# Transposes of k ahead of both of their copies, and the last turned tokens two channel products later

## The chip, the cores and the metric

One core of a Trainium2 chip runs the whole program. The metric is device time in microseconds (us), median of the timed runs. Every run of this study was in the fast state. "The profile" is one execution recorded by the hardware profiler; its engines are PE (TensorE), PEld (TensorE's weight loads), DVE (VectorE), ACT (ScalarE), POOL (GpSimd) and SP. L514 is line 514 of the kernel's source.

## The reference

An RWKV-6 recurrence over 4 batches, 8 heads, 768 steps and head size 48, then an MLP mixer on its result.

```python
for t in range(S):                       # state: (B, H, D, D)
    cur = einsum('bhd,bhe->bhde', u * k[t], v[t])
    y[t] = einsum('bhd,bhde->bhe', r[t], state + cur)
    state = w[t] * state + einsum('bhd,bhe->bhde', k[t], v[t])
x = y as (B, S, H*D)                     # (4, 768, 384)
h = relu(x^T @ w_tok1) @ w_tok2          # tokens, 768 -> 256 -> 768
u = x + h^T
out = u + relu(u @ w_ch1) @ w_ch2        # channels, 384 -> 1536 -> 384
```

## The kernel before

The recurrence is done in 12 units of 256 tokens (two chunks of 128), three units to a batch. A unit's `tokens` transposes k for both chunks (8 transposes, 2 copies); `carry` makes from it the products `kv_ps`, which VectorE adds to the state.

```python
def tokens():                                     # one of the pieces of a unit
    ...
    L["kT"] = apool.tile([128, UC, A, 128], f32, name="kT", bufs=1)
    both = ps_g.tile([128, 2, 512], f32, name="gram").rearrange("p c (a t) -> p c a t", a=A)
    for c in range(UC):                           # UC = 2 chunks, A = 4 pairs of heads
        ps = both[:, c]                           # one PSUM bank for each chunk
        for a in range(A):
            pe.transpose(ps[:, a, :], k_[:, ts(c * A + a, 128)], ident)
        act.copy(L["kT"][:, c], ps)

def carry():
    L, vt = live[i], vs[i]
    kv = L["kv"] = ps_a.tile([128, 2, 512], f32, name="kv_ps", tag="a")
    ...         # pe.matmul(kv[...], L["kT"][...], vt[...])
```

Tiles carry their dependences: whoever reads a tile waits for what was written into it, and a later write waits for an earlier read. `gram` is one tile, with both banks in it.

The mixer of a batch adds the token product to x (`back`), turns 128 tokens of x (`turn`), and multiplies with the channel weights (`up`, 256 tokens at a time, the segment `s`):

```python
def back(c):
    ...         # h_ps = wtok2 x h1
    dve.tensor_add(x[:, c, :], x[:, c, :], ps)                 # L624

def turn(c):
    ...         # ps = xT_ps, in pool "a" in the first and last batch, else a gram tile
    for m in range(DM // 128):
        pe.transpose(ps[:, m, :], xs[bt][:, c, ts(m, 128)], ident)
    act.copy(xT[:, :, ts(c, 128)], ps)

turned = [(1.3, lambda: back(0))]
for c in range(1, C):                             # C = 6
    turned += [(1.3, lambda c=c: back(c)), (0.6, lambda c=c: turn(c - 1))]
turned.append((0.6, lambda: turn(C - 1)))
```

The opening also converts the weights, which come as 64-bit floats, in VectorE steps:

```python
def load():     # sp.dma_start(d64[...], src)     into the tile scratch, L207
def take():
    dve.tensor_scalar(e, top, 0x7FF0, None, op0=ALU.bitwise_and)      # L210, first to read the load
    ...         # L211, L212
def add(): ...                                    # L215
def scale(): ...                                  # L218
def put(): ...                                    # L223
```

And this is how the order on the engines comes about:

```python
for bt in range(B):
    if bt == 0:                                   # units 3 to 5 beside it; a scheduler decides
        to_ch = [whole(e[n < 2:]) for n, e in enumerate(to_ch)]
        late(in_turn[dve.engine], dve, lambda: emit(woven(turned, to_ch[:2])))
        ...
    else:
        hiddens, pieces, ups, downs = mixing(bt)
        pieces = [(c * 0.5, f) for h in hiddens for c, f in h] + [(c * 0.3, f) for c, f in pieces]
        for s in range(S // SEG):
            pieces += ups[s] + downs[s]
    ...
        strict(*(f for _, f in woven(att, pieces)))   # bt 1 and 2: fixed order on PE, DVE and ACT
```

Units 0 to 2 (the opening) and 3 to 5 (beside the first batch's mixer) are ordered in good part by the scheduler, units 6 to 11 (the **woven batches**) by the program. `late(mark, engine, f)` makes an engine's instructions of `f` stand behind `mark` in its queue.

## Time and profile before

| | before |
|---|---|
| device time, median | 601.02 us (600.21 to 602.07, 3 runs) |
| span of the profiled run, its mean granted clock | 603.1 us, 0.977 (this run took 605.13 us, 4.1 above the median) |
| TensorE busy | 565.3 us, 94% |
| VectorE busy | 391.8 us, 65% |
| waits of TensorE's matmuls, 240 to 480 us | 4.9 us, in 8 gaps |

TensorE is the bound, and its gaps are what can be won. The prediction below shows the views that carry this. Two stretches that it doesn't show are needed later. First, TensorE's timeline at the unit with the least to do between the transposes and their reader, `kv_ps`. The columns are start, duration (us), engine, line, operation, out<-in, shape, records in the row, and in brackets the idle time before with what ended it.

```profile
473.58 0.60 PE L514 MATMUL gram<-ident,rk 128*128 128x128 f32 x4
474.86 0.66 PE L514 MATMUL gram<-ident,rk 128*128 128x128 f32 x4 [0.68 <-ACT kT L515]
475.35 1.46 PE L642 MATMUL z_ps<-xT,wch 128*128 128x256 f32 x6
476.74 1.14 PE L524 MATMUL kv_ps<-vt,kT 64*64 64x48 f32 x48
```

Between the first transpose and `kv_ps` lie 3.16 us, 1.28 of them to the second four. Second, VectorE's timeline in the opening, where the mixer of the first batch begins (the same columns):

```profile
86.97 1.22 DVE L218 SCALAR_TENSOR_TENSOR scratch<-scratch 128x1024 f32<-128x1024 f32 x1
88.11 0.68 DVE L343 TENSOR_TENSOR decay<-w 112x512 f32<-112x512 f32 x1
88.71 0.55 DVE L624 TENSOR_TENSOR x<-x,h_ps 128x384 f32<-128x384 f32 x1
89.17 1.28 DVE L223 SCALAR_TENSOR_TENSOR wch<-x,scratch 128x512 uint32<-128x512 uint32 x2
90.38 0.55 DVE L624 TENSOR_TENSOR x<-x,h_ps 128x384 f32<-128x384 f32 x1
90.84 0.69 DVE L210 TENSOR_SCALAR scratch<-scratch 128x1024 uint16<-128x1024 uint16 x1
```

The first two sums into x (L624) come ahead of the first step (L210) of the next conversion, and nothing waits. TensorE's first transposes of x follow the first sum at 89.31 us.

### The profile page before, as it was taken

The numbers are of one execution on the slowest core, as the hardware profiler recorded it, in microseconds if no ns is written. First come the engines' busy times: TensorE is split into PE (matmuls) and PEld (weight loads), VectorE is DVE, ScalarE is ACT, GpSimd is POOL, SyncE is SP. The second block draws the span as 40 slices with busy tenths as digits, with TensorE's granted clock in tenths as the row PEclk, the third lists the DMA queues.
The fourth block names the chain that finished last, engine by engine and source line by source line (L and its number), as shares of the span: only waits on it lengthen the run. The fifth ranks groups of instructions, "written<-read, shape, count | busy, mean of one in ns | idle before, by whom it ended". The sixth has DMA issues, their size and how long they took to land.

```text
span 603.1 us, 17493 instructions
## 1 busy us (share of the span) xinstructions
PE 565.3 (94%) x7828; PEld 483.0 (80%) x7828; DVE 391.8 (65%) x729; ACT 180.1 (30%) x452; POOL 9.3 (2%) x46
## 2 busy tenths in 40 slices
PE   3767899999999999999999999999999999999997
PEld 2757657776897886689898896789899886898987
DVE  5779599998785696577778865677867142040403
ACT  6154435432224422322223302322313212303020
POOL 4000000000010000000000000000000000000000
PEclk9997599989999999999999999999999999999999
DMA  8525555630223315113232122010110000000000
GB/s 340 194 69 158 158 150 190 192 107 2 80 82 86 90 42 171 27 32 104 79 107 80 28 82 79 1 54 16 41 54 28 1 27 0 1 18 10 26 1 26
DMA packets 22969, 45.74 MB, mean 76 GB/s; under 512 B 2512, under 2 KB 14928, under 8 KB 22896
## 3 DMA queue, kind: packets, MB, share of 16 engines
q1 hardware_dynamic: 22752, 44.64, 23.6%
q8 instruction: 61, 1.00, 0.7%
q14 instruction: 12, 0.10, 0.1%
q10 hardware_dynamic: 144, 0.00, 0.0%
HBM read 39.91 MB, written 4.72 MB: 74 GB/s over the span
## 4 chain that ended last, share of the span: by engine, by line
PE 81%; DVE 11%; issue 3%; ACT 3%; DMA 2%; SPq 0%; DVEq 0%; ACTq 0%
PE z_ps L642 29%; PE q_ps L676 23%; PE h_ps L622 5%; PE h_ps L615 4%; PE gram L308 4%; PE gram L386 3%; PE kv_ps L524 2%; PE y_ps L576 2%; PE h_ps L652 2%; DVE rk L342 2%; PE gram L514 2%; PE y_ps L563 2%; PE xT_ps L634 1%; PE gram L302 1%; DMA x<-in_w_ch_dram 1%
## 5 line engine op out<-in xcount | busy, mean ns | idle before, releaser
L642 PE MATMUL z_ps<-xT,wch 128*128 128x256 f32 x864 | 196.3, 384 | 2.0 <-ACT z L644 2.0
L642 PEld LDWEIGHTS z_ps<-xT,wch 128*128 128x128 f32 x864 | 162.6, 191 | 25.3 <-ACT z L644 3.0
L644 ACT ACTIVATE z<-z_ps 128x256 f32<-128x256 f32 x144 | 55.0, 383 | 181.6 <-PE z_ps L642 181.4
L676 PE MATMUL q_ps<-wch,z 128*128 128x192 f32 x528 | 93.4, 328 | 0.0
L676 PEld LDWEIGHTS q_ps<-wch,z 128*128 128x128 f32 x528 | 86.5, 190 | 1.3
L676 PE MATMUL q_ps<-scratch,z 128*128 128x192 f32 x396 | 69.3, 328 | 0.0
L676 PEld LDWEIGHTS q_ps<-scratch,z 128*128 128x128 f32 x396 | 64.6, 190 | 0.4
L308 PEld LDWEIGHTS gram<-rk 48*64 48x64 f32 x1536 | 33.4, 171 | 9.3 <-issue 4.3
L308 PE MATMUL gram<-rk 48*64 48x32 f32 x1536 | 35.7, 250 | 5.4 <-issue 2.6
L342 DVE TENSOR_TENSOR rk<-rk,decay 112x1024 f32<-112x1024 f32 x24 | 29.4, 1223 | 16.1 <-PE gram L302 9.9
L720 DVE TENSOR_TENSOR z<-z 128x768 f32<-128x768 f32 x9 | 8.6, 953 | 47.4 <-ACT z L644 47.4
L412 DVE COPY_PREDICATED at<-mask,gram 128x384 f32<-128x384 uint8 (+2 forms) x72 | 34.5, 481 | 1.4
L622 PE MATMUL h_ps<-h,wtok 128*128 128x384 f32 x96 | 35.0, 491 | 0.0
L615 PE MATMUL h_ps<-x,wtok 128*128 128x384 f32 x96 | 35.0, 518 | 0.0
L624 DVE TENSOR_TENSOR x<-x,h_ps 128x384 f32<-128x384 f32 x24 | 13.2, 551 | 31.4 <-PE h_ps L622 31.4
L342 DVE TENSOR_TENSOR rk<-rk,w 112x1024 f32<-112x1024 f32 x24 | 29.3, 1223 | 6.3 <-PE gram L308 6.1
L615 PEld LDWEIGHTS h_ps<-x,wtok 128*128 128x128 f32 x96 | 18.7, 201 | 11.5 <-issue 0.6
L622 PEld LDWEIGHTS h_ps<-h,wtok 128*128 128x128 f32 x96 | 16.5, 190 | 9.8 <-ACT h L617 2.6
L514 PE MATMUL gram<-ident,rk 128*128 128x128 f32 x96 | 17.0, 305 | 7.6 <-ACT kT L515 7.1
L580 ACT COPY x<-y_ps 128x384 f32<-128x384 f32 x12 | 5.7, 479 | 59.2 <-PE y_ps L576 59.2
L544 DVE TENSOR_TENSOR state<-state,kv_ps 128x192 f32<-128x192 f32 x40 | 14.1, 353 | 11.7 <-PE kv_ps L524 10.5
L686 DVE TENSOR_TENSOR o<-x,z 128x192 f32<-128x192 f32 x11 | 3.9, 355 | 27.2 <-ACT z L685 27.2
(110 smaller groups left out, 650.5 us busy)
## 6 DMA issues: line engine op xcount, KB each, us to landing
rk<-in_rkw_dram SPq DMA_DIRECT2D x36, 192.0 KB, 3.4
x<-in_w_ch_dram SPq DMA_DIRECT2D x10, 512.0 KB, 4.5
vt<-in_v_dram SPq DMA_DIRECT2D x12, 384.0 KB, 4.3
out_dram<-o SPq DMA_DIRECT2D x24, 192.0 KB, 1.9
rp<-in_near_dram SPq DMA_DIRECT2D x12, 384.0 KB, 3.6
scratch<-in_w_ch_dram SPq DMA_DIRECT2D x8, 512.0 KB, 4.7
w<-in_rkw_dram SPq DMA_DIRECT2D x18, 192.0 KB, 3.6
rk<-in_rkw_dram SPq DMA_DIRECT2D x6, 512.0 KB, 6.5
```

The costliest lines, as they stand in the source:

```text
L308: fours(lambda q, j, rows, cols: pe.matmul(g[cols, q, ts(ca, 32)], k_[rows, ds(ca * 128 + j * T, T)], right[rows, ts(2 * ca + j, 32 // b), ...
L342: dve.tensor_mul(halves, halves, by)
L386: fours(lambda q, j, rows, cols: pe.matmul(g[cols, q, ts(a, 96)], k_[rows, ds((c * A + a) * 128 + j * T, T)], L["far", c][rows, ts(2 * a + ...
L412: dve.copy_predicated(out=to[:, :, :, (q + 1) * b:], data=got[:, :, :, first * b:first * b + n], mask=masks4[l][:, q].unsqueeze(1).unsquee ...
L514: pe.transpose(ps[:, a, :], k_[:, ts(c * A + a, 128)], ident)
L544: dve.tensor_add(new, new, got)
L615: pe.matmul(sums[i], wtok1[:, c, ts(i, 128)], xs[bt][:, c, :], start=(c == 0), stop=(c == C - 1))
L622: pe.matmul(ps, wtok2[:, i, ts(c, 128)], h1[:, i, :], start=(i == 0), stop=(i == DTOK // 128 - 1))
L624: dve.tensor_add(x[:, c, :], x[:, c, :], ps)
L642: pe.matmul(ps, wch1[:, m, ts(jt, 128)], xT[:, m, ts(s, SEG)], start=(m == 0), stop=(m == DM // 128 - 1))
L644: act.activation(zs[s][:, jt, :], ps, AF.Relu)
L676: pe.matmul(ps, a[:, j, :], b[:, j, :], start=(j == 0), stop=(j == HJ - 1))
```

## The change

Part one: all eight transposes of a unit are issued, then both copies, so that TensorE doesn't stand between the two fours. Part two: in the woven batches, the last turned tokens of a batch come after two channel products that don't need them, so that VectorE has time to finish the last sum into x.

```diff
             for c in range(UC):
-                ps = both[:, c]
                 for a in range(A):
-                    pe.transpose(ps[:, a, :], k_[:, ts(c * A + a, 128)], ident)
-                act.copy(L["kT"][:, c], ps)
+                    pe.transpose(both[:, c, a, :], k_[:, ts(c * A + a, 128)], ident)
+            for c in range(UC):
+                act.copy(L["kT"][:, c], both[:, c])
@@
             pieces = [(c * 0.5, f) for h in hiddens for c, f in h] + [(c * 0.3, f) for c, f in pieces]
+
+            *pieces, last = pieces
+            ups[0].insert(2, last)
             for s in range(S // SEG):
```

## The prediction

> **What bounds the kernel now.** I began with the busy shares on the page of the kernel before, then read its chain of work that ended last, then its groups.
>
> ```profile
> PE 565.3 (94%) x7828; PEld 483.0 (80%) x7828; DVE 391.8 (65%) x729; ACT 180.1 (30%) x452; POOL 9.3 (2%) x46
> ...
> PEclk9997599989999999999999999999999999999999
> ...
> PE 81%; DVE 11%; issue 3%; ACT 3%; DMA 2%; SPq 0%; DVEq 0%; ACTq 0%
> ...
> L514 PE MATMUL gram<-ident,rk 128*128 128x128 f32 x96 | 17.0, 305 | 7.6 <-ACT kT L515 7.1
> ```
>
> TensorE (PE) is busy 94% of the span and holds 81% of the chain that ended last. From about 150 us on its granted clock is full. So an idle TensorE gap removed after that point should shorten the run one for one, unless the gap comes back elsewhere. The last line is the group the change is about: 96 transposes of k (12 units of 8), before which TensorE sat idle 7.6 us, 7.1 of it for the ScalarE copy kT.
>
> Next I asked for TensorE's waits between 240 and 480 us alone, the two batches in which attention and mixer are woven in a fixed order. The columns are total us, times, longest.
>
> ```profile
> PE gram L514 <- ACT kT L515: 4.1, 6, 0.7
> PE xT_ps L634 <- DVE x L624: 0.8, 2, 0.4
> ```
>
> These are the only two waits that the answer names for the matmul row, and the change aims at exactly these two. Now the timeline of TensorE around one of them (start, duration, what, idle before):
>
> ```profile
> 378.19 0.49 PE L634 MATMUL xT_ps<-ident,x 128*128 128x128 f32 x3
> 378.52 0.60 PE L514 MATMUL gram<-ident,rk 128*128 128x128 f32 x4
> 379.80 0.66 PE L514 MATMUL gram<-ident,rk 128*128 128x128 f32 x4 [0.68 <-ACT kT L515]
> 380.29 1.46 PE L622 MATMUL h_ps<-h,wtok 128*128 128x384 f32 x4
> ...
> 383.20 0.49 PE L634 MATMUL xT_ps<-ident,x 128*128 128x128 f32 x3
> 384.10 0.52 PE L634 MATMUL xT_ps<-ident,x 128*128 128x128 f32 x3 [0.41 <-DVE x L624]
> 384.46 2.76 PE L642 MATMUL z_ps<-xT,wch 128*128 128x256 f32 x12
> ```
>
> Four transposes are issued, then TensorE stands until the first copy has ended, then the other four follow. Five microseconds later the last three token transposes of the batch stand until VectorE has added the last product to x.
>
> **What the Trainium skill says.** (1) "PSUM — Partial Sum Buffer", section "PSUM bank collisions raise a hardware error", has as its rule: "Semaphore-guard PSUM by bank × quadrant (by bank is the simple version), not by address." The tile of the transposes is two banks, one per chunk, so the second four write a bank that the first copy doesn't read. The chip does not ask for this wait; it comes from the dependences being taken for the tile as a whole. The order listing of the changed program agrees: the second four lose their wait on ScalarE, and the first copy now waits for all eight. (2) "TensorE: Matmul & The Clock Gate", section "Part 4: PE-mode transpose", gives about 275 ns for one transpose in a kernel. The trace has 272 to 273 ns as the median of L514, so it agrees; but in a row they start 0.11 us apart (three from 378.19 to 378.52), and this spacing is what counts here. (3) "Perfetto Trace Analysis", section "Identifying Performance Opportunities" (its Optimization Strategy): consistent bubbles, the same gap repeating on the engine that should be saturated, are to be looked for. The 0.68 us above repeats in five of the six units and is 0.73 in the sixth.
>
> **Part one, transposes ahead of both copies.** It adds and removes no instruction. Start to start, the second four follow the first four by 1.33 us once and by 1.28 us five times in the woven batches, 7.73 us in all. Four transposes at 0.11 need 0.44, 2.6 us for six units. So 7.73 - 2.6 gives **5.1 us** of gap. All of it is on TensorE at full clock.
>
> Does it come back at kv_ps (L524), which reads both copies? A copy takes 0.58 us and starts 0.07 us after the last transpose ends, so both are done about 1.2 us later, some 2.3 us after the first transpose starts. Eight transposes take 0.9 us, and the order listing puts between them and kv_ps at least one z_ps group: six records at 0.216 us, 1.3 us, and 0.33 us of issue that kv_ps shows anyway. That is 2.5 us, so no wait in the woven batches, narrowly in the unit at 473 us and widely in the others.
>
> In the first batch's second half (units at 160, 185 and 213 us) other products already lay between the two fours, so there was nearly no wait to lose. There the listing leaves only four q_ps matmuls (two records each, 0.16 us a record, 1.3 us) after the eight. At 160 us I expect about nothing. At 213 us the copies now stand behind two rp copies that wait for VectorE until about 214.6 us, so kv_ps comes with fewer products done: a loss of **0.5 us**.
>
> The opening is different. Timeline of the third unit, all engines:
>
> ```profile
> 69.36 1.11 PE L514 MATMUL gram<-ident,rk 128*128 128x128 f32 x4
> 70.94 0.58 ACT L515 COPY kT<-gram 128x512 f32<-128x512 f32 x1
> 71.58 1.12 PE L514 MATMUL gram<-ident,rk 128*128 128x128 f32 x4 [1.10 <-ACT kT L515]
> 72.73 0.58 ACT L515 COPY kT<-gram 128x512 f32<-128x512 f32 x1 [1.21 <-PE gram L514]
> 73.91 1.95 PE L524 MATMUL kv_ps<-vt,kT 64*64 64x48 f32 x48
> 75.93 0.35 DVE L544 TENSOR_TENSOR state<-state,kv_ps 128x192 f32<-128x192 f32 x1 [6.08 <-PE kv_ps L524]
> ```
>
> Here even VectorE stands 6.08 us for this path, so it is the chain. With eight transposes at 0.18 us each (the lower clock of this stage) the last ends near 71.1, the copies at 71.7 and 72.3, and kv_ps starts at 72.35 instead of 73.91: **1.5 us**. The first unit (40 us) has a 1.15 us gap, but VectorE is busy without a break from 40 to 54 us except 0.23 us there; the second (48 us) has 0.73 us, but what follows waits for a state that VectorE delivers at 49.9 us either way. I count nothing for these two.
>
> **Part two, the last turned tokens later.** Between the two threes at 383.20 and 384.10 lie 0.90 us; three transposes need 0.33. That is 0.57 us, and the same at 250.19 and 251.09: **1.1 us** for two batches. In the first and last batch the scheduler had already put z_ps in between, with no wait, so nothing is to be won. The first channel products read only the first 256 tokens, so they need not wait for the last 128. The delayed copy xT lands behind four rp copies on ScalarE, and the gram tile it frees is wanted 0.3 us after that by my reckoning: no wait, but not by much.
>
> **Sum.** 5.1 + 1.1 + 1.5 - 0.5 = 7.2 us. 601.0 - 7.2 = **593.8 us**, 1.2% less.
>
> **Rivals.** *The wait moves to kv_ps or to the gram tile.* The copies begin later by four transposes, and ScalarE does two in a row. For it: kv_ps already waits for kT four times, 1.9 us in all. Against it: those are not in the six gaps, and the 1.3 us of z_ps cover it. If every woven unit gave back 0.4 us and each batch's delayed transpose 0.3, some 3 us would be lost: about 597. *The opening gives nothing,* because conversions of the weights on VectorE and their loads bound it: the chain has a 6.1 us weight load at 113 us, and the DVE digits are 7 to 9 there. Against it: that load is issued when VectorE frees its buffer, so it would move along. Then about 595.3. *More is won,* as in the first unit's gap and the second half of the first batch, where the chain changes engines often: 1 to 2 us more, 592. *The throttle:* the clock digits 7 and 5 lie at 45 to 75 us; if a denser opening moves them, a microsecond either way.
>
> **Range and chances.** 591.0 to 597.0 holds the sum, its loss to the first rival and the gain of the third. Faster by 2% would need 12 us, more than all waits that the change touches, so 0.04. Slower by 2% needs a new stall of 19 us against the sum, and the order listing shows no such thing: 0.01. Within 2%: 0.95.
>
> **What would show it.** Right: in the profile after, the group of transposes has no idle time for kT between 240 and 480 us, eight of them start within 0.9 us, kv_ps shows only its 0.33 us of issue, and the xT_ps wait for VectorE is gone; busy time of TensorE is unchanged and the span is 7 us shorter, of it 3 in each woven batch. The state update at 75.93 us comes near 74.4. Wrong: a new wait of kv_ps for kT or of gram (L386) for xT in the woven batches, or an opening that ends at the same time as before.

## The result, and the profile after

The changed kernel took **594.92 us** (594.44 to 596.74, 4 runs), the kernel before in the same rounds 601.55 us (600.21 to 602.26, 4 runs). The ratio is 0.9898, interval 0.9870 to 0.9926: 1.0% less time, which counts as the same at 2%. Ratios here are the mean time of one kernel's fast runs over that of the other's of the same rounds, so not quite the ratio of the quoted medians. Sent again later with five rounds, the change gave 0.9878 (0.9848 to 0.9909).

From the page after: busy times, granted clock in 40 slices, chain that ended last.

```profile
PE 564.4 (95%) x7828; PEld 486.0 (82%) x7828; DVE 392.3 (66%) x729; ACT 179.6 (30%) x452; POOL 9.5 (2%) x46
...
PEclk9999998999999999999999999999999999999999
...
PE 81%; DVE 11%; issue 3%; DMA 2%; ACT 2%; SPq 0%; DVEq 0%; ACTq 0%
```

The work is the same, 7828 records and 564 us of it; the chain has the same owners. What went is idle time. TensorE's waits of the matmul row between 240 and 480 us, after (total us, times, longest):

```profile
PE y_ps L563 <- DVE state L544: 0.2, 1, 0.2
```

All eight gaps of before are gone, and one of 0.2 us is new. TensorE's timeline after, at the first woven unit and the end of that batch's turning:

```profile
243.81 1.04 PE L513 MATMUL gram<-ident,rk 128*128 128x128 f32 x8
244.68 1.46 PE L622 MATMUL h_ps<-h,wtok 128*128 128x384 f32 x4
...
247.59 0.49 PE L634 MATMUL xT_ps<-ident,x 128*128 128x128 f32 x3
247.92 2.75 PE L642 MATMUL z_ps<-xT,wch 128*128 128x256 f32 x12
250.51 0.49 PE L634 MATMUL xT_ps<-ident,x 128*128 128x128 f32 x3
250.93 1.15 PE L524 MATMUL kv_ps<-vt,kT 64*64 64x48 f32 x64
```

Eight transposes go through in 0.87 us, and the last three of x stand behind twelve records of `z_ps`. At the narrow unit (473.58 us before):

```profile
466.08 1.04 PE L513 MATMUL gram<-ident,rk 128*128 128x128 f32 x8
466.96 1.46 PE L642 MATMUL z_ps<-xT,wch 128*128 128x256 f32 x6
468.35 1.13 PE L524 MATMUL kv_ps<-vt,kT 64*64 64x48 f32 x48
```

First transpose to `kv_ps` is 2.27 us instead of 3.16, so the gap did not come back there. (The weight load of `kv_ps` does wait 0.33 us for the copies, at 468.35 us in PEld's row, but `z_ps` keeps TensorE busy meanwhile.) In the opening, timelines of TensorE and VectorE put together, after:

```profile
69.30 1.97 PE L513 MATMUL gram<-ident,rk 128*128 128x128 f32 x8
72.48 1.43 PE L524 MATMUL kv_ps<-vt,kT 64*64 64x48 f32 x48
73.99 0.35 DVE L544 TENSOR_TENSOR state<-state,kv_ps 128x192 f32<-128x192 f32 x1 [4.13 <-PE kv_ps L524]
...
85.03 1.22 DVE L218 SCALAR_TENSOR_TENSOR scratch<-scratch 128x1024 f32<-128x1024 f32 x1
88.63 0.69 DVE L210 TENSOR_SCALAR scratch<-scratch 128x1024 uint16<-128x1024 uint16 x1 [2.38 <-DMA scratch<-in_w_ch_dram]
89.24 0.55 DVE L624 TENSOR_TENSOR x<-x,h_ps 128x384 f32<-128x384 f32 x1
89.84 0.57 PE L634 MATMUL xT_ps<-ident,x 128*128 128x128 f32 x3 [2.69 <-DVE x L624]
90.22 2.75 PE L622 MATMUL h_ps<-h,wtok 128*128 128x384 f32 x4
```

The state update comes at 73.99 us instead of 75.93. But at 88 us there is something that before doesn't have. The scheduler, given other transposes, has put L210 **ahead** of the first sum into x (and moved the decay step L343, which stood there, behind it), and L210 waits 2.38 us for a load. VectorE takes its queue in order ("Perfetto Trace Analysis", section "Per-engine timelines", calls ScalarE and VectorE "strict FIFO", and this trace agrees), so the sum waits behind it although its own data is there, and TensorE stands 2.69 us for the sum. Then four records of `h_ps` take 2.75 us instead of the 1.46 that four such records take in before and, after, from 95 us on. So what the opening won may be lost again here.

To say how much, all traces were cut at the same five instructions: first transpose of k; first product of `h_ps` by w_tok2 (L622 in before); sixth `xT_ps` of the first batch; third `xT_ps` of the second batch; first `xT_ps` of the last batch. This table is read off the timelines of TensorE, one look for each row (us). The columns from the start to the end add up to the span. A look is one run: that of before took 605.13 us, those of the change 596.74 and 596.53, the slowest of their sets. So differences of spans are not differences of medians.

| kernel | start | **opening** | **turning**, first batch | rest of first batch | **woven** batches | end | span |
|---|---|---|---|---|---|---|---|
| before | 40.1 | 46.1 | 11.5 | 147.4 | 259.8 | 98.2 | 603.1 |
| the change | 40.1 | 44.2 | 15.4 | 143.8 | 253.0 | 98.2 | 594.7 |
| the change again | 39.3 | 42.9 | 17.1 | 144.1 | 253.0 | 98.2 | 594.5 |
| e1 transposes only | 37.8 | 44.1 | 15.5 | 144.5 | 254.3 | 98.2 | 594.4 |
| e2 turned only | 38.9 | 46.4 | 11.5 | 145.6 | 258.4 | 98.3 | 599.1 |
| e3 woven only | 39.6 | 46.6 | 10.9 | 144.9 | 253.0 | 98.3 | 593.4 |
| e4 opening only | 37.6 | 42.9 | 13.3 | 144.9 | 259.8 | 98.2 | 596.7 |
| e9 opening, order mended | 37.8 | 42.0 | 11.5 | 145.7 | 259.8 | 98.1 | 594.9 |
| e5 change, order mended | 38.5 | 42.1 | 11.5 | 144.6 | 253.0 | 98.3 | 588.0 |
| e5 again | 37.6 | 42.8 | 11.5 | 145.0 | 253.0 | 98.2 | 588.2 |
| e6 copies twice | 38.2 | 42.7 | 15.0 | 143.6 | 255.2 | 98.2 | 592.8 |
| e7 filled between | 38.1 | 46.5 | 10.9 | 147.4 | 252.8 | 98.2 | 593.9 |
| e8 other order alone | 37.6 | 46.5 | 12.5 | 145.8 | 259.8 | 98.2 | 600.5 |
| e10 wait filled | 37.6 | 42.0 | 14.4 | 147.0 | 254.3 | 98.2 | 593.6 |

Start and the rest of the first batch scatter by 2 to 4 us from look to look. The woven stretch doesn't: it is set by the program's order (in e10 alone it has an extra gap of 1.1 us, at 272 us, for which the profile shows no cause). Of the 6.7 us won there, part one has 5.5 (e1) and part two 1.3 (e2).

### The profile page after: what moved, and what is told of

Same layout as the page of the kernel before. It is cut to its first block, busy times and chain, and to the rows that moved or that the text cites. A ratio compares the mean times of both kernels' runs of the same rounds, so it can differ in the third digit from the quotient of the medians.

```text
span 594.7 us, 17493 instructions
## 1 busy us (share of the span) xinstructions
PE 564.4 (95%) x7828; PEld 486.0 (82%) x7828; DVE 392.3 (66%) x729; ACT 179.6 (30%) x452; POOL 9.5 (2%) x46
## 4 chain that ended last, share of the span: by engine, by line
PE 81%; DVE 11%; issue 3%; DMA 2%; ACT 2%; SPq 0%; DVEq 0%; ACTq 0%
PE z_ps L642 28%; PE q_ps L676 23%; PE h_ps L622 5%; PE h_ps L615 4%; PE gram L308 4%; PE gram L386 3%; PE kv_ps L524 3%; PE y_ps L576 2%; PE gram L513 2%; PE y_ps L563 2%; PE h_ps L652 2%; DMA scratch<-in_w_ch_dram 1%; PE gram L302 1%; DVE scratch L218 1%; DVE rk L342 1%
## 5 line engine op out<-in xcount | busy, mean ns | idle before, releaser
L642 PE MATMUL z_ps<-xT,wch 128*128 128x256 f32 x864 | 194.1, 381 | 0.8 <-ACT z L644 0.8
L308 PEld LDWEIGHTS gram<-rk 48*64 48x64 f32 x1536 | 35.3, 177 | 8.9 <-issue 4.3
L308 PE MATMUL gram<-rk 48*64 48x32 f32 x1536 | 37.7, 256 | 5.1 <-issue 2.6
L342 DVE TENSOR_TENSOR rk<-rk,decay 112x1024 f32<-112x1024 f32 x24 | 29.4, 1224 | 15.5 <-PE gram L302 9.9
L622 PE MATMUL h_ps<-h,wtok 128*128 128x384 f32 x96 | 36.4, 507 | 0.0
L624 DVE TENSOR_TENSOR x<-x,h_ps 128x384 f32<-128x384 f32 x24 | 13.3, 552 | 31.5 <-PE h_ps L622 31.5
L615 PEld LDWEIGHTS h_ps<-x,wtok 128*128 128x128 f32 x96 | 18.2, 195 | 11.1
L622 PEld LDWEIGHTS h_ps<-h,wtok 128*128 128x128 f32 x96 | 17.2, 197 | 10.0 <-ACT h L617 2.6
L285 PE MATMUL gram<-rp,kp 48*64 48x64 f32 x384 | 10.4, 271 | 10.1 <-ACT kp L273 7.9
```

Source lines behind the costliest of these rows:

```text
L308: fours(lambda q, j, rows, cols: pe.matmul(g[cols, q, ts(ca, 32)], k_[rows, ds(ca * 128 + j * T, T)], right[rows, ts(2 * ca + j, 32 // b), ...
L342: dve.tensor_mul(halves, halves, by)
L615: pe.matmul(sums[i], wtok1[:, c, ts(i, 128)], xs[bt][:, c, :], start=(c == 0), stop=(c == C - 1))
L622: pe.matmul(ps, wtok2[:, i, ts(c, 128)], h1[:, i, :], start=(i == 0), stop=(i == DTOK // 128 - 1))
L642: pe.matmul(ps, wch1[:, m, ts(jt, 128)], xT[:, m, ts(s, SEG)], start=(m == 0), stop=(m == DM // 128 - 1))
```

## The experiments

Twelve runs were made, of eleven kernels, all with the reference's results. e1 to e4 shared one chip and one set of rounds; so did e5 to e7; so did the change again, e5 again, e9 and e8; e10 ran alone. "Before" is from the same rounds. By the 2% rule all count as the same, but for e5 again, which is unclear; what follows speaks of smaller differences and goes by the intervals.

| kernel | median us (range, runs) | ratio to before, 95% |
|---|---|---|
| e1 | 595.92 (592.43 to 597.29, 6) | 0.9904, 0.9875 to 0.9933 |
| e2 | 600.52 (598.78 to 601.58, 14) | 0.9985, 0.9973 to 0.9997 |
| e3 | 594.94 (593.78 to 596.37, 6) | 0.9899, 0.9877 to 0.9922 |
| e4 | 600.20 (598.80 to 601.71, 22) | 0.9986, 0.9975 to 0.9997 |
| e5 | 590.74 (589.94 to 593.04, 4) | 0.9841, 0.9823 to 0.9860 |
| e6 | 594.84 (593.52 to 595.55, 5) | 0.9903, 0.9888 to 0.9918 |
| e7 | 595.28 (593.76 to 598.54, 6) | 0.9916, 0.9895 to 0.9936 |
| change again | 593.41 (591.31 to 596.53, 6) | 0.9878, 0.9848 to 0.9909 |
| e5 again | 589.97 (589.20 to 591.54, 5) | 0.9822, 0.9798 to 0.9846 |
| e9 | 597.67 (596.41 to 600.22, 21) | 0.9945, 0.9931 to 0.9958 |
| e8 | 601.62 (600.06 to 604.66, 22) | 1.0008, 0.9990 to 1.0026 |
| e10 | 597.88 (595.00 to 600.17, 13) | 0.9937, 0.9917 to 0.9956 |

Before had medians of 600.95 (e1 to e4), 600.92 (e5 to e7), 601.08 (change again, e5 again, e9, e8) and 601.52 us (e10).

### Each part alone: e1 and e2

e1 is the change without part two:

```diff
-            *pieces, last = pieces
-            ups[0].insert(2, last)
```

> Only the first part of the change: all transposes of k ahead of both copies, in all twelve units. My theory: the six woven gaps of TensorE are worth what the trace showed (5.4 us there), the opening nothing net; so 5 to 6 us below the kernel before, and 1.2 us above the full change. Rival (the opening gives 1.5 us, as I predicted, and the woven part less): the same sum here, so this run sizes part one but does not tell the two apart.

e2 is the change with `tokens` as before:

> Only the second part: the last three token transposes of a batch two channel products later. My theory: 0.6 us in each of the two woven batches, 1.2 us below the kernel before, with no idle of xT_ps for VectorE in the woven batches. Rival: the late copy xT makes gram wait for its tile and gives it back; then within 0.3 us of the kernel before.

e1 is 0.96% below before, 5.8 us. e2 is 0.15%, 0.9 us, a little under what was expected; its woven stretch is 1.3 us shorter, as the two gaps of 0.6 us say. In e1's trace the wait of part two is still there (0.41 us at 377.16), in e2's the six of part one. The parts are independent: 5.5 and 1.3 give 6.8 in the woven stretch, and together they won 6.7.

### Where in the run: e3 and e4

e3 is the change with the new order of transposes from unit 6 on; e4 is before with the new order in units 0 to 2 alone:

```diff
-            for c in range(UC):                   # e3: the new loops stand under this if
+            if i >= NEAR:                         # NEAR = 6; e4: if i < UB, UB = 3
+                ...                               # eight transposes, then two copies
+            else:
+                ...                               # as before
```

> Both parts, but the transposes ahead of the copies only in units 6 to 11, the woven ones; units 0 to 5 as before, so the scheduler's order of the opening is the old one. My theory: the opening's win at kv_ps is given back at about 88 us where VectorE waits for a weight load, so this is within 0.7 us of the full change (6 to 7 us below the kernel before). Rival (the opening gives 1.5 us net): 1.5 us or more above the full change, 5 us below the kernel before.

> Transposes ahead of the copies only in the first three units, nothing else changed. My theory: kv_ps of the third unit about 1.4 us earlier, then a wait of VectorE for a load of a weight of over 2 us ahead of its first sum into x near 88 us, and in the time 0 against the kernel before, within 0.7 us. Rival: 1.5 us below the kernel before.

e3's ratio is 0.9899, the change's was 0.9898, but 0.9878 when sent again. So by time the new order in units 0 to 5 is worth between 0 and 1.3 us net, with intervals of 0.2 to 0.3% on each ratio, and the 1.0 us that the prediction counts there (1.5 - 0.5) is not ruled out. e4 is 0.8 us below before (0.2 to 1.5), a little more than expected. Its trace shows both sides of the account: its opening is 3.2 us shorter than that of before, its turning 1.8 us longer. VectorE, e4:

```profile
84.36 0.69 DVE L210 TENSOR_SCALAR scratch<-scratch 128x1024 uint16<-128x1024 uint16 x1 [1.85 <-DMA scratch<-in_w_ch_dram]
84.97 0.55 DVE L631 TENSOR_TENSOR x<-x,h_ps 128x384 f32<-128x384 f32 x1
```

### The order of VectorE in the opening: e5, e9 and e8

Theory: the opening does get faster by the change, and the place of L210 takes it back. e5 is the change, with the second conversion of the channel weights kept behind the second sum into x, as it was before:

```diff
+            added = []
+            turned[1] = (turned[1][0], lambda f=turned[1][1]: (f(), added.append(newest(dve))))
+            to_ch[1] = (to_ch[1][0], lambda f=to_ch[1][1]: late(added[0], dve, f))
             late(in_turn[dve.engine], dve, lambda: emit(woven(turned, to_ch[:2])))
```

> The full change, and in the opening the second weight conversion kept behind the second sum into x on VectorE, as it stood in the kernel before. My theory: the wait of VectorE for the load of a weight no longer stands ahead of the first sum, TensorE's 2.7 us wait at the first xT_ps is gone, and the opening's win of 1.5 us at kv_ps is kept in part: 1 to 2 us below the full change, about 593.5. Rival (the opening is bound by the loads and conversions as a whole, and the order only moves the wait): within 0.5 us of the full change.

VectorE's timeline of e5:

```profile
82.44 0.68 DVE L343 TENSOR_TENSOR decay<-w 112x512 f32<-112x512 f32 x1
83.04 0.55 DVE L624 TENSOR_TENSOR x<-x,h_ps 128x384 f32<-128x384 f32 x1
84.71 0.55 DVE L624 TENSOR_TENSOR x<-x,h_ps 128x384 f32<-128x384 f32 x1
85.17 0.69 DVE L210 TENSOR_SCALAR scratch<-scratch 128x1024 uint16<-128x1024 uint16 x1
```

And TensorE's, at the first transposes of x:

```profile
83.64 0.55 PE L634 MATMUL xT_ps<-ident,x 128*128 128x128 f32 x3 [0.22 <-DVE x L624]
84.03 1.46 PE L622 MATMUL h_ps<-h,wtok 128*128 128x384 f32 x4
```

The wait is gone, without one work instruction more or less; the load lands while VectorE does what it can. The turning takes 11.5 us, as in before. The time is 1.6% below before, and more below the change than the expected 1 to 2 us. To compare it with the change itself, both were sent together:

> The full change once more, on the same chip as the next three. 594 to 596.5 us; its trace again with VectorE idle about 2 us for the weight load ahead of the first sum into x, and the woven batches 6.7 us shorter than in the kernel before.

> The change with the second conversion behind the second sum, beside the change on one chip. My theory: 2.5 to 4.5 us below the change, with no wait of VectorE for the load. Rival (the 4 us between two sittings were chip or throttle): within 1 us of the change.

589.97 against 593.41 us on one chip: 3.4 us, as expected (the change itself came out 0.6 below its expected 594). e9 puts the same three lines on e4:

> The kernel before with the transposes ahead of the copies in the first three units only, as in e4_opening_only, and with the conversion kept behind the second sum. My theory: what e4_opening_only gave back comes through, 2.5 to 4 us below the kernel before (e4_opening_only: 0.75 us). Rival (opening bound by loads whatever the order): under 1.2 us.

e9 is 0.55% below before, 3.3 us, as expected, where e4 was 0.8. What the three lines do to the kernel before, where L210 stands behind the second sum anyway, was not run. So the new order in the opening is worth about 3.3 us, and the displaced L210 took 2.5 of it in e4. e8 goes the other way: the kernel before, with L210 split off and put ahead of the first sum.

```diff
+            first_ch, bits = to_ch[0], to_ch[1][1]            # bits: L210 of the second conversion
+            ...
+            late(in_turn[dve.engine], dve, lambda: emit((0, f) for f in (*first_ch[1:4], bits)))
+            turned[0] = (turned[0][0], lambda f=turned[0][1], mark=newest(dve): late(mark, dve, f))
```

> The kernel before with the other order alone: the first step of the second conversion ahead of the first sum into x on VectorE, transposes as before. My theory: VectorE waits for the load there, about 1 to 2 us since it comes to that place some 2 us later than in the changed kernel, and the time is 1 to 2 us above the kernel before. Rival: within 0.5 us.

This expectation was missed, and its rival came: 0.5 us slower (0.6 less to 1.6 more), within the noise. VectorE, e8:

```profile
86.05 0.69 DVE L356 TENSOR_TENSOR decay<-w 112x512 f32<-112x512 f32 x1
87.70 0.69 DVE L230 TENSOR_SCALAR scratch<-scratch 128x1024 uint16<-128x1024 uint16 x1 [0.96 <-DMA scratch<-in_w_ch_dram]
88.31 0.55 DVE L637 TENSOR_TENSOR x<-x,h_ps 128x384 f32<-128x384 f32 x1
```

The wait came, but only 0.96 us of it, and the turning is 1.0 us longer than in before. The load is issued when a step L223 of VectorE has freed its tile, so it moves along with VectorE, and the time from its issue is what counts. In the change (issue at 80.46 us) VectorE is free for L210 after 5.8 us, and L210 can start after 8.2. In e8 (issue at 80.35) it is free after 6.4, since one more instruction (L356, the L343 of before) stands in front, and L210 starts after 7.4. So of the 1.4 us between the two waits that instruction has 0.6, and the rest is the load's own time, from one look each. The wrong place costs as much as the load outlasts the work in front of L210.

### The margins in the woven batches: e6 and e7

The rival of the prediction was that the wait moves to `kv_ps`. e6 doubles ScalarE's copies in the woven batches, e7 keeps the two fours apart but puts other products between them (and leaves units 0 to 5 as before, but for a slip: the unit at 208 us does its second four and their copy twice, so the trace has 100 transposes of k instead of 96; this lies outside the woven stretch):

```diff
             for c in range(UC):                                   # e6
-                act.copy(L["kT"][:, c], both[:, c])
+                for _ in range(2 if i >= NEAR else 1):
+                    act.copy(L["kT"][:, c], both[:, c])
```

```diff
-        pieces = [..., (0.3, tokens[1]), (1.9, begin[1]), far0, far1, ...                                   # e7
+        pieces = [..., (0.3, tokens[1]), (1.9, begin[1]), (0.3, lambda: fours_of[i](1)), far0, far1, ...
```

> The full change with each copy kT done twice in units 6 to 11 (same result), 1.07 us of ScalarE more ahead of kv_ps in each. My theory: only the unit that has a single z_ps group between the transposes and kv_ps (at 466 us, no slack left) pays, about 1.1 us; the other five have 4 us of products in between and pay nothing: 0.8 to 1.5 us above the full change. Rival (the copies sit on the path in every unit, through the relu of z_ps or the gram tile): 4 us or more above.

> The full change, except that in units 6 to 11 the two fours of transposes with their copies are kept as before the change but with products of the mixer put between them. My theory: the wait is worth only the idle TensorE, so filling it does as well as taking it away: within 1 us of the full change. Rival (eight transposes in a row gain by themselves, or a shorter path to kv_ps matters): some 5 us above the full change.

TensorE's timeline of e6 at the narrow unit:

```profile
463.06 1.04 PE L513 MATMUL gram<-ident,rk 128*128 128x128 f32 x8
463.94 1.46 PE L643 MATMUL z_ps<-xT,wch 128*128 128x256 f32 x6
466.50 1.14 PE L525 MATMUL kv_ps<-vt,kT 64*64 64x48 f32 x48 [1.10 <-ACT kT L516]
```

Two more copies are 1.2 us of ScalarE there, and 1.1 of it shows. So the margin of this unit is about 0.1 us, as narrow as the prediction called it. The woven stretch is 2.1 us longer, some more than the expected 0.8 to 1.5: three other units lose 0.36 us each, which was not expected. The timed median (594.84) doesn't show this, but it was not taken beside the change and the openings scatter by more; what e6 costs in time is left open. e7's woven stretch is 252.8 us, 0.2 below the change. Filling the wait or taking it away comes to the same; that the two are equal says that nothing but the gap was lost there.

### Is the slow stretch after the wait part of its cost? e10

In the traces where TensorE stood at the first transposes of x, the four records of `h_ps` right after were slow: 2.75 us after 2.69 us of idleness (the change), 2.69 after 2.76 (e1), 2.77 after 3.08 (the change again), 2.23 after 2.29 (e6). They took 1.46 us after 2.16 (e4), 1.60 (e8) and 0.22 (before, e5). The view by stretches gives the granted clock of the change from 89.80 to 93.40 us as 0.56, and of e5 from 83.60 to 87.70 as 1.00. "TensorE: Matmul & The Clock Gate", section "Why this matters for your kernels", warns of idle gaps over about 3 us between matmul bursts, after which the clock falls to half. e10 tried to test it, with needless products in the wait:

```diff
+            if (bt, c) == (0, 0):
+                for _ in range(8):
+                    pe.matmul(ps[:, 0, :], ident, ident, start=True, stop=True)
             for m in range(DM // 128):
                 pe.transpose(ps[:, m, :], xs[bt][:, c, ts(m, 128)], ident)
```

> The whole change, with eight needless products of the identity with itself (128 x 128, into the tile xT_ps that the first transposes of x overwrite) put on TensorE just ahead of the first transposes of x, that is into the wait near 88 us. The results stay right. The traces so far show TensorE's granted clock at about half after that wait where it was long: the four records of h_ps right behind the first xT_ps took 2.75 us after 2.69 us of idleness, 2.69 after 2.76, 2.77 after 3.08, 2.23 after 2.29, but 1.46 after 2.16, 1.60 and 0.22. THEORY: the idleness itself lowers the clock, so the wait for the load costs more than its own length. Then, with the products (estimated 0.11 us each, from the spacing of the transposes, 0.9 us in all) the idleness left in one piece is under 2.2 us, the four records take 1.46 us again and the granted clock there is 1.00, although VectorE still waits some 2.4 us for the load and the first xT_ps comes no earlier. RIVAL: the low clock comes from something else of that time (the dense opening before it, the loads), then the four records take 2.2 to 2.8 us here too. TIME: the scheduler moved one sum into x behind one conversion step and other products in the first batch, so the time is only a side witness: 0 to 1.5 us below the change by the theory, the same by the rival.

TensorE's timeline of e10:

```profile
82.38 1.95 PE L635 MATMUL xT_ps<-ident 128*128 128x128 f32 x16
84.16 0.54 PE L637 MATMUL xT_ps<-ident,x 128*128 128x128 f32 x3
84.54 1.46 PE L622 MATMUL h_ps<-h,wtok 128*128 128x384 f32 x4
```

The records took 1.46 us, as the theory has it. But the test doesn't decide: VectorE waited only 1.31 us for the load in this look, and after so short a wait e8 kept its clock without any filling. The products were also twice as long as estimated. The time (597.88) is no witness either, since a sum into x had moved behind conversion steps and TensorE lost 0.99 us at 88.72 to it. Other gaps in the kept traces speak against a length of some 2.2 us that decides. TensorE's timelines of before and of e7:

```profile
121.32 11.02 PE L642 MATMUL z_ps<-xT,wch 128*128 128x256 f32 x42 [2.01 <-ACT z L644]
220.68 1.52 PE L386 MATMUL gram<-rp,rk 48*64 48x96 f32 x32 [1.33 <-DVE w L393]
```

The granted clock is 0.50 from 122.20 to 125.50 us in before, after a wait of 2.01 us, and from 220.80 to 224.20 in e7, after 1.33, where in e4 it stayed 1.00 after 2.16. So the length of the last wait alone doesn't tell whether the clock falls. What does is open.

## Why the prediction was right

593.8 us were predicted, 594.9 measured, 593.4 when sent again. The sum was right. Three of its four terms held; the opening was wrong in its mechanism, and that the sum came so near all the same is in part luck.

1. **The six gaps of part one, 5.1 us: right.** First to second four was 1.3 us and is part of 0.9 us for all eight. The woven stretch of e1 is 5.5 us shorter. That the chip would let the first copy run beside the second four, as the prediction takes from the PSUM page, no run here shows: in all traces no copy of kT overlaps a transpose of k.
2. **No new wait at kv_ps, "narrowly in the unit at 473 us": right,** and e6 shows the margin, about 0.1 us. It rests on two copies of 1.07 us together beside 1.46 us of `z_ps`. The first rival (about 597) fell with that. The gram tile's margin held too: no wait at L386.
3. **Part two, 1.1 us: right.** 1.3 us in e2's woven stretch, 0.9 in its time.
4. **The unit at 213 us, a loss of 0.5 us: right by itself,** for `kv_ps` waits there:

```profile
214.10 1.08 PE L524 MATMUL kv_ps<-vt,kT 64*64 64x48 f32 x46 [0.55 <-ACT kT L515]
```

   From the first transpose of that unit to the next `y_ps` (L563) it was 8.50 us and is 9.11. All the same the rest of the first batch is not longer: six looks with the new order in units 3 to 5 have 143.6 to 145.0 us there, seven with the old one 144.9 to 147.4 (e10, which has 147.0 with the new order, left out). The two of 147.4, before and e7, each hold one of the stretches at half clock shown above; the other five with the old order have 144.9 to 145.8. Why the new order is rather shorter by about one is open; single looks scatter here by as much.
5. **The opening, 1.5 us: wrong in its size and in its fate.** "I count nothing for these two" was the step that failed first: the path isn't only the third unit's. Over all traces the opening is 46.1 to 46.6 us with the old order (five looks) and 42.0 to 44.2 with the new (nine): 3.6 us between the means, and 3.3 in the time of e9. Of the 3.6, 1.3 come before the third unit's transposes (though none of it in the change's first look), 1.4 between these and `kv_ps`, as predicted (72.48 instead of 73.91), and 0.9 after it. A part of this may be the throttle, which the prediction had as a rival worth a microsecond: the granted clock is back at full 36.0 to 39.5 us after the first transpose of k with the old order and 29.8 to 33.1 with the new. Whether the new order brings that about, no run separates. What failed next is the assumption that the gain is kept from there on. The scheduler changed VectorE's order 15 us later, and the turning grew by 3.9 us in the change and by 5.5 in its repetition. So in both looks opening and turning together end later than in before, at 99.7 and 99.2 us against 97.8, which meets the prediction's own sign of being wrong: "an opening that ends at the same time as before". In time the net worth was 0.8 us in e4 and between 0 and 1.3 in the change against e3. The prediction's second rival (the opening gives nothing, "because conversions of the weights on VectorE and their loads bound it", 595.3) is nearest to this, but with another cause: the load bounds nothing as long as VectorE is not made to wait for it with the sum behind it (e5).

So the gain that the prediction counted for the opening was won, more than twice over, and mostly lost again for a reason that the prediction didn't have; the woven part was a little larger than counted. The order listing that I had read for TensorE and ScalarE also shows L210 ahead of L624 on VectorE (the trace after has the same order; the listing is not in the record); the prediction makes no use of it, for the change doesn't name VectorE.

The best version is e5: 590.0 us, 3.4 below the change on the same chip, 11.1 below before (1.8%; whether it is 2% is unclear, the interval goes from 1.5 to 2.0).

## What to carry to other kernels

If a fixed-order stretch shows the same short gap again and again because one tile is half written and half read, issue all writes and then all reads; count first whether enough other work lies before the reader (here 1.46 us beside 1.07 us of copies). Where a scheduler decides the order, look at the order of every engine after a change, not only of those that the change names: an instruction that waits for a load, put one place too early in an in-order queue, took back 3.4 us here, and three lines that fix its place gave them back. Cut the traces of all kernels at the same few instructions, and a stretch that gains is told from one that loses even where the total comes out as predicted.

## What the Trainium skill lacked or had wrong

- "TensorE: Matmul & The Clock Gate", section "Part 4: PE-mode transpose", gives one transpose's duration (about 275 ns, beside a figure for bf16; 272 to 273 here in fp32), not the spacing in a row, which is what counts for time; the page's spacings of back-to-back products are not for fp32 transposes. Here eight pass in 0.87 us, 0.11 us each at full clock.
- The same page's section "Why this matters for your kernels" puts the gap after which the clock falls at about 3 us. Here the granted clock fell to 0.50 after a wait of 2.01 us (before, 121 us) and of 1.33 (e7, 221 us), and four records took 2.23 us instead of 1.46 after 2.29 (e6); after 2.16 us (e4) they did not. One look each, and the cause is not isolated.
- "Perfetto Trace Analysis", section "Identifying Performance Opportunities", gives for consistent bubbles one possible reason, that SBUF or PSUM doesn't suffice for the next tile. Here the same gap of 0.68 us came from one tile with two banks being taken as one dependence, and no buffer was added to remove it.
- No page that I read gives how a load's wait in VectorE's queue spreads: 2.38 us on VectorE became 2.69 us on TensorE and, with the slower clock after it, 3.9 us of a stretch of 11.5.
- None gives the scatter of one program in the fast state: the change ran from 591.3 to 596.5 us in one set of rounds, with mean granted clocks of 0.977 to 1.0 that do not order the times. These means can lack a stretch: the profile of the change gives 1.00 from 45 to 72 us, where eight transposes of k took 1.97 us (at 69.30) against 1.04 in the woven batches.
